# Hash attention and MLP on one Trainium2 core: attention by whole head pairs in place of half pairs

## The chip, the cores and the metric

The kernel runs on one core of one Trainium2 chip (trn2). The metric is device time in microseconds (us) of one execution, from the start of the program to its end; lower is better. The engines are called PE (TensorE, matrix products), DVE (VectorE), ACT (ScalarE), POOL (GpSimd) and SP (SyncE, which here only issues DMAs). SBUF is the on-chip memory, and PSUM is where PE writes its results; it has eight banks of 512 f32 columns on 128 partitions.

## The reference

Two stages follow each other. The first is attention with a mask by hash: each query and key gets six bits, the signs of its products with `proj`, and a query sees only the keys of its own bucket. The second is an MLP with PReLU over the attention's output, reshaped to 3072 tokens of 512.

```python
# q, k, v: (4, 8, 768, 64) f32; proj: (64, 6); w_in: (512, 2048); w_out: (2048, 512)
q_bits = (np.einsum('bhsd,dk->bhsk', q, proj) > 0)
k_bits = (np.einsum('bhsd,dk->bhsk', k, proj) > 0)
mask = q_bucket[:, :, :, None] == k_bucket[:, :, None, :]
scores = np.where(mask, scale * np.matmul(q, k.transpose(0, 1, 3, 2)), -1e9)
attn = np.exp(scores - scores.max(-1, keepdims=True))
attn = attn / (np.sum(attn, axis=-1, keepdims=True) + 1e-09)
x = np.matmul(attn, v)          # then (B,H,S,D) -> (B*S, H*D)
h = x @ w_in
out = (np.maximum(h, 0.0) + alpha * np.minimum(h, 0.0)) @ w_out
```

## The kernel before

The kernel has a fast path (`fast_path`) that always runs, and a general path that runs afterwards only if a flag says that the inputs were out of range; it doesn't run here. All that follows is the fast path. It has an attention stage of about 345 us and an MLP stage (a Winograd-like scheme of seven products in place of eight) of about 550 us.

Attention works on **head pairs**: two heads of 64 lie side by side on the 128 partitions, and there are 4 x 4 = 16 pairs. The 768 queries of a pair are cut into `NCH` = 2 chunks of `CW` = 384, and the 768 keys into `NC` = 6 blocks of 128. A **unit** `u` is one chunk of one pair (32 units); each of its steps is a function:

- `turn` (L671): six PE transposes bring q or k of a pair from tokens on partitions to head dimensions on partitions (`tr`); one copy by ACT takes them out of PSUM.
- `hash_bits` (L691): PE multiplies `tr` by `wh`, which holds `proj` in 32 columns for each head's 64 rows; each product takes the 64 rows of one head and writes 32 partitions. ACT takes the signs (DVE for k in the first pair) and writes `bits` as bf16: for each pair four instructions of 32 rows for q and three of 64 or 128 rows for k. The heads' and halves' places in PSUM are crossed (`s ^ half`), so that the eight products of a pair stand in eight different places of PE's array.
- `scores` (L730): a tile is 128 keys by 384 queries for both heads. The bit products go first (bf16, both heads side by side in PE's rows), and q times k in f32 is added to them in PSUM. ACT takes the exponential of the tile, 128x768, into one of ten `pt` tiles (L742). A key outside the bucket gets so small an exponent that its share vanishes. `two_banks` (L666) gives the PSUM tile; there are three, shared by scores, turns and bits.
- `add_first`, `add_last`, `add_total` (L749 to L760): the sum of the six `pt` tiles of a unit, tile by tile. DVE adds tiles 0 and 1 into `accp`; a DMA issued by POOL adds tile 2 to it in place; DVE adds tiles 3, 4 and 5 into `accd`, and `accp` to that.
- `attend` (L763): v transposed times the exponentials, in 32-column pieces, into one PSUM bank `av`. In chunk 0 one more column of ones gives the sum of v.
- `totals` (L776): a product of `accd` with ones gives each query's sum in a bank of its own, `sm`.
- `divide` (L786): DVE transposes these sums, takes reciprocals, POOL copies them between partitions, DVE spreads them by a second transpose and multiplies `av` by them (L811); the result `x` is stored to DRAM (`x_s`).

Beside that, attention prepares the weights: the 32 pieces of `w_in` and `w_out` come as 64-bit words and are rounded to f32 by `weight_abs` (ACT), `weight_clamp`, `weight_parts`, `weight_sum` and `weight_sums` (DVE), one piece per unit, and stored to DRAM for the MLP.

**What sets the order.** `do` keeps the compute instructions of every engine in the order in which the program calls them. The loop over units (from L1123 on) calls: the second half of this unit's score tiles, the first half of the next unit's, `divide` of the previous unit with the weight work inside it, the additions, bits of the next pair (first chunk) or turns for the pair after it (second chunk), `attend`, `totals`. So PE has six score tiles, one block of bits or turns, one v product and one block of sums per unit. DMAs are not held by `do`: the framework places those of SP and POOL on their queues by its own schedule. The tiles of `tile_pool` with `bufs=1` or 2 set which write waits for which read.

PSUM has three score tiles of two banks, one bank `av` and one bank `sm`. In the MLP, class `Product` uses `two_banks` for its bank "a", and the banks of `sm` and `av` for "b" and "c".

Of the kernel before, what the change touches and what calls it, by code (L numbers as in the profile page):

```python
# [406 lines left out]
def fast_path(  # L407
# [41 lines left out]
    attn = ctx.enter_context(ExitStack())  # L449
    pool = attn.enter_context(tc.tile_pool(name="sb", bufs=2))  # L450
# [3 lines left out]
    UNITS = NPAIR * NCH  # L454
# [4 lines left out]
    ones = const.tile([P, 32], F32, name="ones")  # L459
    wh = const.tile([P, 32], F32, name="wh")  # L460
# [6 lines left out]
    qbs = [pool.tile([P, S], BF16, name=f"qb{i}", bufs=1) for i in range(2)]  # L467
# [9 lines left out]
    NPT = 10  # L477
    pts = [pool.tile([P, 2, CW + 1], F32, name=f"pt{i}", bufs=1) for i in range(NPT)]
    n_pt = [0]

    nat, tr, bits = {}, {}, {}
    prob, accp, accd, av, vsum, sums = {}, {}, {}, {}, {}, {}
# [21 lines left out]
    def setup():  # L504
# [4 lines left out]
        for s in range(2):  # L509
            nc.sync.dma_start(wh[D * s : D * s + D, :NB], proj)  # L510
        nc.sync.dma_start(alpha16, moe_alpha.rearrange("(t p) -> t p", p=P))
        make_identity(nc, ident)
        do(DVE.memset(ones, 1.0))

        ps = psum.tile([P, 512], F32, name="nil", tag="av")
        nil.append(lambda: do(PE.matmul(ps, zero[:, :P], zero, start=True, stop=True)))
# [4 lines left out]
        for r in range(0, P, 32):  # L521
            do(DVE.memset(hb[r : r + 2 * NB], 1.0 if r % D else -1.0))
            do(DVE.memset(hb[r : r + NB], -1e-37))
# [5 lines left out]
        for t in pts:  # L529
            do(POOL.memset(t[:, :, CW : CW + 1], 1.0))  # L530
        for t in qbs:
            do(POOL.memset(t, 0.0))
# [158 lines left out]
    def hash_bits(pi, halves=BOTH, engine=None):  # L691

        if halves.start == 0:
            bits["q", pi] = qbs[pi % 2]
            bits["k", pi] = pool.tile([P, S], BF16, name=f"kb{pi}", tag="kb")
        ps = {"k": two_banks(f"hs{pi}")}
        ps["q"] = psum.tile([P, 1, 512], F32, name=f"hsq{pi}", tag="sm") if engine is DVE else ps["k"]
        for half in range(halves.start, halves.stop):  # L700
            for name in "qk" if engine is DVE else "kq":
                for s in range(2):
                    r, c = D * s, D * (s ^ half) + 32 * "kq".index(name)

                    for t, c in [("k", c)] + ([("q", c ^ D)] if engine is DVE and name == "q" else []):
                        do(PE.matmul(
                            ps[t][c : c + 32, half if t == "k" or engine is not DVE else 0, :CW], wh[r : r + D],
                            tr[name, pi][r : r + D, half * CW : (half + 1) * CW], start=True, stop=True,
                        ))
        for half in range(halves.start, halves.stop):  # L710
            cols = slice(half * CW, (half + 1) * CW)
            for s in range(2):
                c = D * (s ^ half ^ (engine is DVE)) + 32
                do(ACT.activation(  # L714
                    bits["q", pi][D * s : D * s + 32, cols], ps["q"][c : c + 32, 0 if engine is DVE else half, :CW], AF.Sign, bias=hb[c : c + 32],
                ))

            for to, c, n in [(0, 0, P)] if half == 0 else [(0, D, D), (D, 0, D)]:
                dst, src = bits["k", pi][to : to + n, cols], ps["k"][c : c + n, half, :CW]
                if engine is DVE:  # L720
                    do(DVE.tensor_scalar(
                        dst, src, hb_k[c : c + n, 0:1], hb_k[c : c + n, 1:2], op0=ALU.is_gt, op1=ALU.subtract,
                    ))
                else:
                    do(ACT.activation(dst, src, AF.Sign, bias=hb[c : c + n]))  # L725


    def scores(u, half):
        pi, g = divmod(u, NCH)
        qs = slice(g * CW, (g + 1) * CW)  # L730
        for kc in range(half * NC // 2, (half + 1) * NC // 2):
            sc = two_banks(f"sc{u}_{kc}")
            ks = slice(kc * P, (kc + 1) * P)
            for what, first in ((bits, True), (tr, False)):
                for s in range(2):
                    r = slice(D * s, D * s + D)
                    do(PE.matmul(  # L737
                        sc[:, s, :CW], what["k", pi][r, ks], what["q", pi][r, qs], start=first, stop=not first,
                    ))
            pt = pts[n_pt[0] % NPT]  # L740
            n_pt[0] += 1
            do(ACT.activation(pt[:, :, :CW], sc[:, :, :CW], AF.Exp, scale=SCALE / DOWN))  # L742
            prob[u, kc] = pt


    def p(u, kc):
        return prob[u, kc][:, :, :CW]

    def add_first(u):  # L749
        accp[u] = pool.tile([P, 2, CW], F32, name=f"accp{u}", tag="accp")  # L750
        do(DVE.tensor_tensor(accp[u], p(u, 0), p(u, 1), op=ALU.add))  # L751
        nc.gpsimd.dma_start(accp[u], p(u, 2), accum_op=ALU.add)  # L752

    def add_last(u):
        accd[u] = pool.tile([P, 2, CW], F32, name=f"accd{u}", tag="accd", bufs=1)
        do(DVE.tensor_tensor(accd[u], p(u, 3), p(u, 4), op=ALU.add))  # L756
        do(DVE.tensor_tensor(accd[u], accd[u], p(u, 5), op=ALU.add))  # L757

    def add_total(u):
        do(DVE.tensor_tensor(accd[u], accd[u], accp[u], op=ALU.add))  # L760


    def attend(u):  # L763
        pi, g = divmod(u, NCH)
        av[u] = psum.tile([P, 512], F32, name=f"av{u}", tag="av")
        w = CW + 1 if g == 0 else CW
        for kc in range(NC):
            for s in range(2):
                for t in range(0, D, 32):
                    do(PE.matmul(  # L770
                        av[u][D * s + t : D * s + t + 32, :w], nat["v", pi][:, s, kc * D + t : kc * D + t + 32],
                        prob[u, kc][:, s, :w], start=(kc == 0), stop=(kc == NC - 1),
                    ))


    def totals(u):  # L776

        sums[u] = psum.tile([P, HW2], F32, name=f"sm{u}", tag="sm")
        for s in range(2):
            for h in range(2):  # L780
                r = D * s + 32 * h
                do(PE.matmul(  # L782
                    sums[u][r : r + 32], ones, accd[u][:, s, h * HW2 : (h + 1) * HW2], start=True, stop=True,
                ))

    def divide(u, between=lambda: None):  # L786

        pi, g = divmod(u, NCH)  # L790
        b, hp = pairs[pi]
        if g == 0:
            vsum[pi] = pool.tile([P, 1], F32, name=f"vs{pi}", tag="vs")
            do(DVE.tensor_scalar(vsum[pi], av[u][:, CW : CW + 1], EPS, None, op0=ALU.mult))
        n = HW2 // 32
        a = pool.tile([P, HW2], F32, name=f"st{u}", tag="st", bufs=1)
        r = pool.tile([P, n], F32, name=f"rc{u}", tag="rc")
        rr = pool.tile([P, 2, n], F32, name=f"rr{u}", tag="rr")
        d = pool.tile([P, CW], F32, name=f"dn{u}", tag="dn", bufs=1)
        do(DVE.transpose(a, sums[u]))  # L800
        do(DVE.tensor_scalar(r, a.rearrange("p (n w) -> p n w", w=32)[:, :, 0], S * EPS, None, op0=ALU.add))
        do(DVE.reciprocal(rr, r.unsqueeze(1).to_broadcast([P, 2, n])))  # L802
        for q0 in (0, D):
            q1 = q0 + 32
            do(POOL.tensor_copy(rr[q0 : q0 + 32, 1], rr[q1 : q1 + 32, 1]))  # L805
            do(POOL.tensor_copy(rr[q1 : q1 + 32, 0], rr[q0 : q0 + 32, 0]))  # L806
        between()
        do(DVE.transpose(d, rr.rearrange("p h n -> p (h n)").unsqueeze(2).to_broadcast([P, 2 * n, 32])))

        x = mid.tile([P, CW], F32, name=f"x{u}", tag="x")  # L810
        do(DVE.scalar_tensor_tensor(x, av[u][:, :CW], vsum[pi], d, op0=ALU.add, op1=ALU.mult))  # L811
        nc.sync.dma_start(x_s[b, hp][:, g * CW : (g + 1) * CW], x)
# [25 lines left out]
    class Product:  # L838
# [9 lines left out]
        def times(self, bank, left, right, start):  # L848

            if start:  # L850
# [3 lines left out]
                else:  # L854
                    t = psum.tile([P, 512], F32, name=self.name + bank, tag="sm" if bank == "b" else "av")
# [217 lines left out]
    def verdict():  # L1073
        ps = psum.tile([4, P], F32, name="vd", tag="sm")
# [15 lines left out]

    last = UNITS - 1
    first, second = slice(0, 1), slice(1, 2)
    load_part(0, "q", slice(0, CH), nc.sync)
# [19 lines left out]
    scores(0, 0)  # L1113
# [3 lines left out]
    add_first(0)  # L1117
# [4 lines left out]
    weight_sum(0)  # L1122
    for u in range(UNITS):  # L1123
        pi, g = divmod(u, NCH)

        def weight_rest():
            weight_sum(u)
            weight_group(u)
            weight_clamp(u + 1)

        scores(u, 1)
        if u < last:
            scores(u + 1, 0)
        if u:
# [140 lines left out]
```

## Time and profile before

| what | value |
|---|---|
| time, median of three runs | 900.01 us (899.64 to 900.18) |
| time of the profiled run; span of its trace | 899.33 us; 897.5 us |
| exponentials, L742 | 192 x 813 ns |
| f32 score passes, L737 | 768 x 482 ns |
| v product passes, L770 | 1536 x 488 ns |
| bit passes, L706 | 256 x about 497 ns |
| sum passes, L782 | 256 x 326 ns |
| the three other additions on DVE, L751, L756, L757 | 32 each x 951, 949, 958 ns |
| DMA over the whole span | 146.88 MB, mean 164 GB/s |

An f32 product is two passes on PE, each of which the profile counts. A row of the profile's groups has the line, engine, operation, result and operands, shape, count, then busy time and the mean of one, then the engine's idle time ahead of it and what ended it. For PE a form such as 64*128 is the part of the array that a pass takes, rows by columns; passes in different parts run at the same time, and their recorded durations overlap, so PE's rates are read from start to start.

### The profile page before, as it was taken

To read this page: it belongs to the slowest core of one execution; us is meant where nothing else is said; L and a number is where in the kernel's file an instruction comes from. 1 tells how busy PE (TensorE), PEld (TensorE's weight loads), DVE (VectorE), ACT (ScalarE), POOL (GpSimd) and SP (SyncE) were. 2 spreads that over 40 slices of the span, in tenths; PEclk is the share of its full clock that TensorE was granted. 3 is DMA by queue.
4 is the path that set the end of the run, shared out by engine and by line. 5 is a ranking of instruction groups with operands and counts; after the bars stand their busy time and mean duration, and the time that the engine had idled before them with its cause. 6 is when DMAs were issued, how large, how long until landed. Compare 5 with 4: busy or idle time off the path is not lost.

```text
span 897.5 us, 15668 instructions
## 1 busy us (share of the span) xinstructions
PE 886.4 (99%) x5886; PEld 590.7 (66%) x5886; DVE 757.3 (84%) x1362; ACT 406.2 (45%) x726; POOL 100.4 (11%) x194
## 2 busy tenths in 40 slices
PE   9999999999999999999999999999999999999996
PEld 4444445444444445557997557997557998556996
DVE  5988988988999996899988668988668989768986
ACT  6788888888888863222112222112222111222111
POOL 1222222222232222120000000000000000000000
PEclk9999999999999999999999999999999999999999
DMA  9778888699799765478333535343525242530242
GB/s 240 183 179 184 209 222 214 169 269 275 170 233 212 186 159 175 174 275 304 123 130 99 171 98 179 101 152 86 173 97 192 95 158 78 155 120 0 95 144 71
DMA packets 131909, 146.88 MB, mean 164 GB/s; under 512 B 78304, under 2 KB 118000, under 8 KB 128240
## 3 DMA queue, kind: packets, MB, share of 16 engines
q1 hardware_dynamic: 118672, 123.90, 44.5%
q0 software_dynamic: 11008, 20.97, 11.7%
q8 instruction: 48, 0.79, 0.4%
q10 hardware_dynamic: 2144, 0.92, 0.4%
q14 instruction: 37, 0.30, 0.1%
HBM read 104.87 MB, written 28.31 MB: 148 GB/s over the span
## 4 chain that ended last, share of the span: by engine, by line
PE 89%; DVE 7%; DMA 2%; issue 1%; SPq 1%; ACT 0%; DVEq 0%; ACTq 0%
PE sc L737 17%; PE av L770 14%; PE f_0a L858 2%; PE z_3a L858 2%; PE z_6a L858 2%; PE z_5a L858 2%; PE f_2a L858 2%; PE f_1a L858 2%; PE z_2a L858 2%; PE f_3a L858 2%; PE z_7a L858 2%; PE z_1a L858 2%; PE z_4a L858 2%; PE f_7a L858 2%; PE f_6a L858 2%; PE f_5a L858 2%
## 5 line engine op out<-in xcount | busy, mean ns | idle before, releaser
L742 ACT ACTIVATE pt<-sc 128x768 f32<-128x768 f32 x192 | 153.6, 813 | 48.5 <-PE sc L737 46.7
L737 PE MATMUL sc<-qT,kT 64*128 64x384 f32 x768 | 155.2, 482 | 0.0
L770 PE MATMUL av<-pt,vn 128*32 128x384 f32 (+1 forms) x1536 | 130.6, 488 | 0.5 <-DVE x L811 0.5
L770 PEld LDWEIGHTS av<-pt,vn 128*32 128x32 f32 x1536 | 46.6, 109 | 75.7 <-issue 71.1
L737 PEld LDWEIGHTS sc<-qT,kT 64*128 64x128 f32 x768 | 68.2, 188 | 35.8 <-issue 35.6
L911 DVE TENSOR_TENSOR g<-g,g 128x384 f32<-128x384 f32 x128 | 68.4, 555 | 2.2
L737 PE MATMUL sc<-qb,kb 64*128 64x384 bf16 x384 | 63.3, 324 | 0.1
L752 POOL DMA_DIRECT2D accp<-pt x32 | 38.6, 1205 | 194.3 <-issue 78.6
L975 DVE TENSOR_TENSOR gs<-g,gs 128x768 f32<-128x768 f32 x56 | 53.4, 953 | 1.0
L967 DVE TENSOR_TENSOR ws<-wl 128x512 f32<-128x512 f32 x56 | 38.5, 688 | 17.7 <-DMA wl<-w_out_s 16.1
L975 DVE TENSOR_TENSOR gs<-g 128x768 f32<-128x768 f32 x56 | 53.3, 953 | 0.0
L907 DVE SCALAR_TENSOR_TENSOR g<-h,alpha 128x384 f32<-128x384 f32 x32 | 19.7, 616 | 26.4 <-ACT h L900 26.4
L737 PEld LDWEIGHTS <-kb 64*128 64x128 bf16 x384 | 18.8, 94 | 30.6 <-issue 9.2
L760 DVE TENSOR_TENSOR accd<-accd,accp 128x768 f32<-128x768 f32 x32 | 30.7, 958 | 7.7 <-DMA accp<-pt 6.8
L714 ACT ACTIVATE qb<-hs,hb 32x384 bf16<-32x384 f32 x60 | 34.4, 574 | 1.1
L757 DVE TENSOR_TENSOR accd<-accd,pt 128x768 f32<-128x768 f32 x32 | 30.7, 958 | 3.3
L751 DVE TENSOR_TENSOR accp<-pt,pt 128x768 f32<-128x768 f32 x32 | 30.4, 951 | 0.0
L756 DVE TENSOR_TENSOR accd<-pt,pt 128x768 f32<-128x768 f32 x32 | 30.4, 949 | 0.0
L806 POOL COPY rr<-rr 32x6 f32<-32x6 f32 x64 | 27.5, 430 | 2.6
L805 POOL COPY rr<-rr 32x6 f32<-32x6 f32 x64 | 19.8, 310 | 61.6 <-DVE rr L802 60.3
L725 ACT ACTIVATE kb<-hs,hb 64x384 bf16<-64x384 f32 (+1 forms) x45 | 26.0, 578 | 0.6
L800 DVE STREAM_TRANSPOSE st<-sm 128x192 f32<-128x192 f32 x32 | 12.2, 381 | 14.0 <-PE sm L782 13.8
(350 smaller groups left out, 1824.6 us busy)
## 6 DMA issues: line engine op xcount, KB each, us to landing
wi<-w_in_s SPq DMA_DIRECT2D x32, 896.0 KB, 4.7
wl<-w_out_s SPq DMA_DIRECT2D x16, 1024.0 KB, 4.8
accp<-pt POOLq DMA_DIRECT2D x32, 384.0 KB, 5.2
wl<-w_out_r SPq DMA_DIRECT2D x12, 1024.0 KB, 4.9
raw<-in_moe_w_out_dram SPq DMA_DIRECT2D x16, 512.0 KB, 5.2
raw<-in_moe_w_in_dram SPq DMA_DIRECT2D x16, 512.0 KB, 5.0
w_in_s<-wsi SPq DMA_DIRECT2D x16, 448.0 KB, 5.8
vn<-in_v_dram SPq DMA_DIRECT2D x16, 384.0 KB, 6.0
```

The source lines that it names most:

```text
L714: do(ACT.activation(bits["q", pi][D * s : D * s + 32, cols], ps["q"][c : c + 32, 0 if engine is DVE else half, :CW], AF.Sign, bias=hb[c : ...
L737: do(PE.matmul(sc[:, s, :CW], what["k", pi][r, ks], what["q", pi][r, qs], start=first, stop=not first,))
L742: do(ACT.activation(pt[:, :, :CW], sc[:, :, :CW], AF.Exp, scale=SCALE / DOWN))
L751: do(DVE.tensor_tensor(accp[u], p(u, 0), p(u, 1), op=ALU.add))
L752: nc.gpsimd.dma_start(accp[u], p(u, 2), accum_op=ALU.add)
L757: do(DVE.tensor_tensor(accd[u], accd[u], p(u, 5), op=ALU.add))
L760: do(DVE.tensor_tensor(accd[u], accd[u], accp[u], op=ALU.add))
L770: do(PE.matmul(av[u][D * s + t : D * s + t + 32, :w], nat["v", pi][:, s, kc * D + t : kc * D + t + 32], prob[u, kc][:, s, :w], start=(kc = ...
L858: do(PE.matmul(self.ps[bank], self.left(left, k), self.right(right, k), start=start and k == 0, stop=k == self.nk - 1, skip_group_check=no ...
L911: do(DVE.tensor_tensor(new_g(b, to)[:, i], g_m[b, x][:, i], g_m[b, y][:, i], op=ALU.subtract))
L967: do(DVE.tensor_tensor(t, w2[b, n, x], w2[b, n, y], op=op))
L975: do(DVE.tensor_tensor(t, g2[b, n, x], g2[b, n, y], op=ALU.subtract))
```

## The change

A pair is now one step: the loop runs over 16 pairs and handles both chunks together.

- All 12 score tiles of a pair follow each other, in the order key block by key block with both chunks of each. `pts` is now six tiles, one per key block, which hold both chunks; there is one set of them.
- Then follow both turns for pair + 2, the bits of pair + 1, the v product of both chunks, the sums of both chunks.
- `av` has two banks, one per chunk, from a pool of its own that is closed with the attention stage. The sums no longer have a bank: they go into columns 400 to 495 of `av`'s banks. Each group of 32 partitions takes two quarters of a chunk's sums there, 96 columns each, by two products with `ones` that is one in 16 of its 32 columns and zero in the others, the second added to the first.
- `hash_bits` multiplies all 128 rows at once: `wh` has two versions, each with zeros in the other head's rows. The places are no longer crossed. ACT takes q's signs for both heads and both chunks in one instruction of 128x768, and k's in two of 32x768. The tile with zeros between its bits is now k's (`kbs`), not q's.
- The additions are 1536 wide, four on DVE and one by DMA for each pair; `accp` and `accd` have one buffer each. In `divide` the spreading transpose and the multiply are 768 wide, and x is stored by one DMA.
- Weight work is done for two pieces per pair, spread between these steps.
- In the MLP, banks "b" and "c" come from a new pool that takes the place of `av`'s.

The diff, cut to its core:

```diff
+    psum_av = attn.enter_context(tc.tile_pool(name="psa", bufs=1, space=bass.MemoryType.PSUM))
...
-    pts = [pool.tile([P, 2, CW + 1], F32, name=f"pt{i}", bufs=1) for i in range(NPT)]
+    pts = [pool.tile([P, NCH, 2, CW + 1], F32, name=f"pt{i}", bufs=1) for i in range(NC)]
...
-            nc.sync.dma_start(wh[D * s : D * s + D, :NB], proj)
+            nc.sync.dma_start(wh[D * s : D * s + D, s, :NB], proj)
...
         for half in range(halves.start, halves.stop):
-            for name in "qk" if engine is DVE else "kq":
+            for n, name in enumerate("qk"):
                 for s in range(2):
-                    r, c = D * s, D * (s ^ half) + 32 * "kq".index(name)
...
+                    c = D * s + 32 * n
+                    w = D if engine is DVE and name == "q" else 32
+                    do(PE.matmul(
+                        ps[name][c : c + w, half, :CW], wh[:, s, :w], tr[name, pi][:, half * CW : (half + 1) * CW],
+                        start=True, stop=True,
+                    ))
...
+        do(ACT.activation(
+            cells(bits["q", pi], slice(0, P)), ps["q"][:, halves, :CW], AF.Sign, bias=hb,
+        ))
+        for s in range(2):
+            c = D * s + 32
+            dst, src = cells(bits["k", pi], slice(D * s, D * s + 32)), ps["k"][c : c + 32, halves, :CW]
...
+                do(ACT.activation(dst, src, AF.Sign, bias=hb[c : c + 32]))
...
-            do(ACT.activation(pt[:, :, :CW], sc[:, :, :CW], AF.Exp, scale=SCALE / DOWN))
+            do(ACT.activation(pts[kc][:, g, :, :CW], sc[:, :, :CW], AF.Exp, scale=SCALE / DOWN))
...
+    def add_first(pi):
+        accp[pi] = pool.tile([P, 2 * NCH, CW], F32, name=f"accp{pi}", tag="accp", bufs=1)
+        do(DVE.tensor_tensor(accp[pi], p(0), p(1), op=ALU.add))
+        nc.gpsimd.dma_start(accp[pi], p(2), accum_op=ALU.add)
...
+        for g in range(NCH):
+            for e in range(2):
+                for s in range(2):
+                    for h in range(2):
+                        r = D * s + 32 * h
+                        do(PE.matmul(
+                            av[pi][r : r + 32, g, SUMS : SUMS + QW], ones[:, e],
+                            accd[pi][:, NCH * g + s, h * HW2 + e * QW : h * HW2 + (e + 1) * QW],
+                            start=e == 0, stop=e == 1, skip_group_check=True,
+                        ))
...
+        x = mid.tile([P, NCH, CW], F32, name=f"x{pi}", tag="x", bufs=1)
+        do(DVE.scalar_tensor_tensor(x, av[pi][:, :, :CW], vsum[pi], d, op0=ALU.add, op1=ALU.mult))
+        nc.sync.dma_start(x_s[b, hp], x.rearrange("p g w -> p (g w)"))
...
-                    t = psum.tile([P, 512], F32, name=self.name + bank, tag="sm" if bank == "b" else "av")
+                    t = psum_bc[0].tile([P, 512], F32, name=self.name + bank, tag=bank)
...
+        scores(pi, [c for c in CELLS if pi or c not in ahead])
+        if pi:
+            divide(pi - 1, weight_begin)
+        add_first(pi)
+        weight_sum(i)
+        weight_group(i)
+        load_weight(i + 3)
...
+        weight_clamp(i + 1)
+        add_last(pi)
+        weight_parts(i + 1)
+        weight_sum(i + 1)
+        weight_group(i + 1)
+        load_weight(i + 4)
+        add_total(pi)
+        weight_sums(2)
+        if pi + 2 < NPAIR:
+            turn(pi + 2, "q")
+            turn(pi + 2, "k")
+        if pi + 1 < NPAIR:
+            hash_bits(pi + 1)
+        attend(pi)
+        if pi + 1 == NPAIR:
             now = ff1(0, 0)
             now.step(1)
             now.step(5)
...
+        totals(pi)
+        if pi + 1 == NPAIR:
+            divide(pi)
```

## The prediction, made before the changed kernel was run

> **What bounds the kernel now.** I read the page's busy lines first, then busy time by stretch, then TensorE's (PE's) own waits, and last its order of time through one head pair.
>
> ```profile
> span 897.5 us, 15668 instructions
> PE 886.4 (99%) x5886; PEld 590.7 (66%) x5886; DVE 757.3 (84%) x1362; ACT 406.2 (45%) x726; POOL 100.4 (11%) x194
> ...
> 150.00:317.00 167.00, 167.00 (x1705) 81.31 (x1700) 152.25 (x280) 144.02 (x217) 43.27 (x80) 1.00 0.83 211
> ...
> PE sm L782 <- DVE accd L760: 0.9, 1, 0.9
> PE av L770 <- DVE x L811: 0.5, 1, 0.5
> ```
>
> The stretch 150 to 317 us holds eight head pairs of the attention stage. Its columns are PE, weight loads, VectorE (DVE), ScalarE (ACT), GpSimd (POOL), granted clock, DMA share, GB/s. PE is busy for all of 167.00 us; DVE for 91%, ACT for 86%, DMA for 83%. The last two lines are all that PE waited for in attention once it ran: 1.4 us, both in the first pairs. So the stage lasts as long as PE's instruction stream, and the other three have slack of about 2 to 3 us per pair. A pair takes 167.00/8 = 20.87 us. Its stream (one later half of a pair, then the first half of the next):
>
> ```profile
> 150.09 0.51 PE L782 MATMUL sm<-accd,ones 128*32 128x192 f32 x8
> 150.53 0.34 PE L737 MATMUL sc<-qb,kb 64*128 64x384 bf16 x2
> 150.70 0.81 PE L737 MATMUL sc<-qT,kT 64*128 64x384 f32 x4
> ...
> 154.58 0.33 PE L737 MATMUL sc<-qb,kb 64*128 64x384 bf16 x2
> 155.48 0.88 PE L678 MATMUL tp_q<-ident,qn 128*128 128x128 f32 x6
> ...
> 156.94 4.08 PE L770 MATMUL av<-pt,vn 128*32 128x384 f32 x48
> 160.83 0.51 PE L782 MATMUL sm<-accd,ones 128*32 128x192 f32 x8
> 161.27 0.34 PE L737 MATMUL sc<-qb,kb 64*128 64x384 bf16 x2
> ...
> 166.22 0.51 PE L706 MATMUL hs<-kT,wh 64*32 64x384 f32 x2
> ...
> 166.57 0.49 PE L706 MATMUL hs<-kT,wh 64*32 64x384 f32 x2
> ...
> 167.03 1.18 PE L770 MATMUL av<-pt,vn 128*32 128x385 f32 x12
> ```
>
> Durations overlap, so I use start to start. Six score tiles: 155.48 - 150.53 = 4.95. Turns: 156.94 - 155.48 = 1.46. V product of a chunk: 160.83 - 156.94 = 3.89 (the other chunk 3.90). Sums: 161.27 - 160.83 = 0.44. Bits: 167.03 - 166.22 = 0.81. A pair is 2 x 4.95 + 1.46 + 0.81 + 2 x 3.90 + 2 x 0.44 = 20.85, as found.
>
> Inside a block the rates are plain. A score tile repeats after (154.58 - 150.53)/5 = 0.81. In the v product 48 passes in column groups of 32 go in rounds of four: 3.89/12 = 0.324 per round, which is 0.84 ns a column. The 192-column sums are two rounds of half that, 0.325; the 0.44 shows 0.115 between blocks. Twelve transposes of 128 columns at 0.84 are 1.30, block 1.46: again about 0.12 to 0.16. The bits' 16 passes of 384 columns take only two rounds (starts at 166.22 and 166.57), eight at once.
>
> **What the Trainium skill says.** "TensorEngine Tiling (Array Packing)", section "Tiling Modes", lists 128x32 as four independent tiles and 64x32 as eight. The trace agrees: four v passes per 0.324 us, eight bit passes per 0.33. Its "Key Properties" say that a change of mode drains the array. The trace agrees where it can show it: v product to sums, both 128*32, loses nothing (3.89 is twelve rounds), while each change of mode costs about 0.12. "DMA: Bandwidth & Descriptors", section "Issuing engines are not separate DMA queues", says that all issuers share 16 engines; the DMA share of 0.83 in the stretch fits, and makes the larger accumulating transfer the doubtful one.
>
> **The change, part by part (PE, the path).**
>
> *Bits.* The weight is now 128 rows high with zeros for the other head, so the mode goes from 64*32 to 128*32. The passes stay 16 of 384 columns, but four fit at once: 4 x 0.324 = 1.30 in place of 0.65. Cost +0.65 per pair. Bounds: 0 if eight still ran at once, +0.77 with a drain behind it.
>
> *Order and modes.* Now: scores, turns, v, sums, scores, bits, v, sums: six mode changes. Then: 12 score tiles (64*128), turns (128*128), bits, v, sums (all 128*32): three. Gain 3 x 0.12 = -0.36. Bounds -0.25 (bits to v not seamless) and -0.45.
>
> *Sums.* Sixteen passes of 192 columns become 32 of 96: eight rounds of 0.081 = 0.65, as now 2 x 0.325. Nothing here shows 96 columns; transposes of 128 columns follow at 0.109, their full streaming rate, so weight loads are hidden to that size. At 0.109 a round the cost would be 8 x 0.028 = +0.22. I take 0.
>
> Scores and v product keep passes and shapes: 0. By the blocks: 4.95 + 6 x 0.81 = 9.80, turns 1.46, bits 1.30, v 24 x 0.324 = 7.78, sums 0.65 + 0.115: 21.10 against 20.85, **+0.25 per pair**. Fourteen pairs make bits for the next: +3.5. The last has no bits and saves two changes: -0.2.
>
> **What lies beside it.** Per pair on DVE, four additions of 1536 take the place of eight of 768:
>
> ```profile
> L760 DVE TENSOR_TENSOR accd<-accd,accp 128x768 f32<-128x768 f32 x32 | 30.7, 958 | 7.7 <-DMA accp<-pt 6.8
> ...
> accp<-pt POOLq DMA_DIRECT2D x32, 384.0 KB, 5.2
> ```
>
> The 384-wide addition of the second stage takes 555 ns (its row), so the slope is 1.04 ns a column and 1536 take about 1.75 us: 4 x 0.16 = 0.65 saved. The wider transpose and multiply of the division save some 0.3 more. ACT loses four 32-row and three other sign operations (7 x 0.58) and gets one of 128x768 and two of 32x768 (0.81 each): -1.6. Neither bounds, so this is worth nothing to the span; PE at 167.00 of 167.00 hides it.
>
> The waits are new. Set t = 0 at the pair's first score matmul. DVE: division 0.2 + 2 x (0.38 + 0.17 + 0.23), in it the weight's first half 2.3, then 1.0 + 1.0 for the wide transpose and multiply, to about 6.3 with the start (v's banks are needed at 12.6), first addition to 8.1, weight work to 10.1, two additions to 13.6, weight work to 16.5, total to 18.2. PE wants the sums at 9.80 + 1.46 + 1.30 + 7.78 = 20.3: 2.1 us spare. The accumulating DMA, now 768 KB and 512 packets, may land up to 10.4 us after the first addition before PE waits. It took 5.2 for half, of which POOL's issue was 1.2; doubling all gives 10.4, doubling issue and transfer but not latency some 8. Just inside. On ACT the 12 exponentials at 0.81 keep pace with 0.81 a tile and three buffers; turns and signs follow. Behind them the magnitudes end at about t = 18, and only then may q and k three pairs ahead load; SP issues them beside v and weight loads, with 6 us to landing, at about t = 24 to 26 against a need at 21 + 9.8. POOL's copies precede its DMA and end by t = 4. All hidden, with less room than now.
>
> **Start.** The first bit products on DVE's path are 64 and 32 columns wide in turn (+0.65 each, two calls), and k's signs become two instructions of 0.68 for one: scores start about 1.0 later than the present 8.3. Against that go the two waits above (1.4) and four mode changes. Adding up to the end of the first pair's sums I get 33.4 to 35.4, depending on k of pair 2 and on the first DMA; the same work now ends at about 36.05 less three tiles, 33.6. Take +0.5 (-0.5 to +2).
>
> **End.** The MLP's second bank now comes out of the pair's v banks, free when the division's last multiply ends. From the sums' end that takes 0.25 (release) + 0.8 + 0.8 + 1.0 (POOL) + 1.0 + 1.0 = 4.9 us; PE has three products of 1.29 (3.9) ahead of it. +0.9 (0 to 2). The MLP itself is untouched.
>
> Sum: 3.5 - 0.2 + 0.5 + 0.9 = **+4.7 us** on the span of 897.5. The profiled run's own time was 899.33, the three runs 899.64 to 900.18, so I add it to 900.0: about 904.8.
>
> **Rivals.**
> A, other side: the bits stay cheap. If passes of half-zero 128-row weights also went eight at once, the pair would lose only mode changes: -0.36 to -0.45 and, with 15 pairs, about 895. It decides below a bit block of 1.0 us. For it: 0.65 now. Against it: the v product has the new shape and never shows more than four per 0.324. 6%.
> B, a wait takes over: the doubled accumulating DMA lands later than 10.4 us after the addition. Each microsecond beyond costs 16: landing at 11.5 gives 920. For it: DMA share 0.83, the longest landing 9.9 for half the size, and DVE did wait for it six times (6.8 us). Against: most landings near 5. 12%.
> C, q and k land after the turn wants them: bursts of weight loads in the middle pairs, 2 to 5 us in one to three pairs: 908 to 915. 8%.
> D, no change: start and end come out at their low bounds and drains at 0.15: +1. 8%.
>
> **The numbers.** My case 66%, own range 902 to 909; A 6, B 12, C 8, D 8. 0.2% (1.8 us) is about what a measurement of this kernel can tell from no change. Faster 0.06, same 0.08, slower 0.86. Eight in ten lie between 901.5 and 914: A below, most of B above.
>
> **What would show it.** Bit block at 1.3 us with four passes per round; 12 tiles in 9.8; no gap between bits, v and sums; period 21.1; PE still busy throughout; DVE's share down to some 85%. Wrong if bits take 0.65, or if PE waits for the total, for the banks of v, or for q and k at the turns.

## The result, and the profile after

The changed kernel took 914.1 us (912.8 to 914.96, 6 runs) against 899.83 us before on the same chip (899.34 to 901.17, 6 runs): a ratio of 1.0156, 95% interval 1.0143 to 1.017. It is slower, as forecast, but by 14.3 us and not by 4.7; 914.1 lies just above the range's end of 914.0. The profiled run, 912.8 us, was the fastest of the six; its span grew from 897.5 to 911.0 us, by 13.5, and it is these 13.5 us that the traces explain.

PE's order of time through one pair after the change; columns are start, duration, engine, line, operation, result and operands, part of the array, shape, count:

```profile
160.05 0.34 PE L735 MATMUL sc<-qb,kb 64*128 64x384 bf16 x2
...
169.84 0.88 PE L679 MATMUL tp_q<-ident,qn 128*128 128x128 f32 x6
...
171.30 0.52 PE L706 MATMUL hs<-qT,wh 128*32 128x384 f32 x2
171.31 0.52 PE L706 MATMUL hs<-kT,wh 128*32 128x384 f32 x2
171.65 0.49 PE L706 MATMUL hs<-qT,wh 128*32 128x384 f32 x2
171.66 0.49 PE L706 MATMUL hs<-kT,wh 128*32 128x384 f32 x2
171.97 0.49 PE L706 MATMUL hs<-qT,wh 128*32 128x384 f32 x2
...
172.29 0.49 PE L706 MATMUL hs<-qT,wh 128*32 128x384 f32 x2
...
172.62 3.74 PE L768 MATMUL av<-pt,vn 128*32 128x385 f32 x44
```

Start to start: 12 score tiles 9.79, turns 1.46, bits 1.32 in four rounds (171.30, 171.65, 171.97, 172.29) and the v product right behind the fourth. The pair before gives the rest:

```profile
151.52 7.94 PE L768 MATMUL av<-pt,vn 128*32 128x385 f32 x96
159.27 0.85 PE L784 MATMUL av<-accd,ones 128*32 128x96 f32 x32
```

V product 159.27 - 151.52 = 7.75, sums 160.05 - 159.27 = 0.78. A pair is 9.79 + 1.46 + 1.32 + 7.75 + 0.78 = 21.10 us. The forecast was 21.10, and each of its blocks is within 0.03 us of these. So the steady pair is not where the time went. PE's waits show where it did (waiter, what it waited for, us in total, times, longest), together with the tile `accp`, asked for in the stretch 180 to 215 us:

```profile
PE av L784 <- DVE accd L755: 6.9, 2, 6.6
...
L747 POOL DMA_DIRECT2D accp<-pt x1: 1282/1282/1282, 188.7 to 188.7; - x1
...
  DVE accd L755: 9.5, 1
...
DMA to landing us min/median/max: 17.7/17.7/17.7
```

In pair 8 (counted from 0) the sums (L784) waited for the total, and the total had waited 9.5 us for the accumulating DMA, which was issued at 188.7 and landed 17.7 us later. Over the whole run the median of its landings is 9.3 us. The 6.6 us of PE's wait count from the recorded end of the last v pass; from start to start the sums, which began at 208.23, came 6.8 us late (208.23 - 193.72 - 7.75, where 193.72 is the start of pair 8's v product). What shared the 16 DMA engines with it is in SP's order of time:

```profile
188.62 0.91 SPq L846 DMA_DIRECT2D wi<-w_in_s  x2
189.62 0.43 SPq L568 DMA_DIRECT2D raw<-in_moe_w_in_dram  x1
190.27 0.65 SPq L846 DMA_DIRECT2D wi<-w_in_s  x1
```

These are the first three loads of the MLP's weights, 896 KB each. The program calls two of them in pair 9 and one in pair 12; the framework, which places SP's DMAs by its own schedule, put all three into pair 8, within 2 us of the accumulating DMA. That is not new: the kernel before issues the same three loads one behind the other in the same pair. Here are that line of SP's order of time, and the landings of its four accumulating DMAs (384 KB each) in the stretch 180 to 215 us:

```profile
191.97 7.02 SPq L836 DMA_DIRECT2D wi<-w_in_s  x3
...
DMA to landing us min/median/max: 4.5/7.8/9.9
```

The one issued at 190.5, just ahead of the loads, took 8.5 us to land and the next, at 201.4, took 9.9, the longest of that whole run, against a median of 5.2. PE waited for neither.

In the changed kernel the wait had a sequel. Busy time by stretch (length, then PE, weight loads, DVE, ACT, POOL, clock, DMA share, GB/s):

```profile
201.90:204.00 2.10, 0.00 (x0) 0.00 (x0) 0.00 (x0) 0.02 (x1) 0.00 (x0) 1.00 1.09 318
...
205.50:206.00 0.50, 0.00 (x0) 0.00 (x0) 0.00 (x0) 0.00 (x0) 0.00 (x0) 0.74 1.24 298
206.00:208.00 2.00, 0.00 (x0) 0.00 (x0) 1.58 (x1) 0.00 (x0) 0.00 (x0) 0.50 0.87 197
208.00:212.50 4.50, 4.27 (x44) 2.76 (x46) 2.73 (x13) 0.81 (x1) 1.27 (x4) 0.50 0.36 109
212.50:214.00 1.50, 1.50 (x12) 0.80 (x10) 1.47 (x2) 1.01 (x2) 0.00 (x0) 0.98 0.04 11
```

PE's granted clock falls to one half between 205.5 and 206 and is back at about 212.5. By then PE works again, at half speed: the sums of pair 8 take 1.44 us in place of 0.78, and the next twelve score tiles 11.21 in place of 9.79.

The 13.5 us, from the two traces: start -0.9 (the first pair's sums end at 32.75; the same work ended at 33.6 before), steady pairs and last pair +3.5, wait in pair 8 +6.8, half clock +2.1 (0.66 + 1.42), a wait of 0.5 in pair 2, end +1.5.

### The profile page after: what moved, and what is told of

Same layout as the page of the kernel before. It is cut to its first block, busy times and chain, and to the rows that moved or that the text cites. A ratio compares the mean times of both kernels' runs of the same rounds, so it can differ in the third digit from the quotient of the medians.

```text
span 911.0 us, 15799 instructions
## 1 busy us (share of the span) xinstructions
PE 893.1 (98%) x6134; PEld 603.8 (66%) x6134; DVE 741.6 (81%) x1269; ACT 386.8 (42%) x664; POOL 54.4 (6%) x110
## 4 chain that ended last, share of the span: by engine, by line
PE 52%; DVE 6%; DMA 1%; issue 1%; SPq 0%; ACT 0%; DVEq 0%; POOL 0%; ACTq 0%
PE z_5a L868 2%; PE z_3a L868 2%; PE z_6a L868 2%; PE f_2a L868 2%; PE f_1a L868 2%; PE z_2a L868 2%; PE f_3a L868 2%; PE z_7a L868 2%; PE f_0a L868 2%; PE z_1a L868 2%; PE z_4a L868 2%; PE f_7a L868 2%; PE f_6a L868 2%; PE f_5a L868 2%; PE f_4a L868 2%; PE z_2c L868 1%
## 5 line engine op out<-in xcount | busy, mean ns | idle before, releaser
L768 PE MATMUL av<-pt,vn 128*32 128x385 f32 (+1 forms) x1536 | 127.0, 485 | 0.0
L755 DVE TENSOR_TENSOR accd<-accd,accp 128x1536 f32<-128x1536 f32 x16 | 28.1, 1758 | 27.6 <-DMA accp<-pt 27.6
L751 DVE TENSOR_TENSOR accd<-pt,pt 128x1536 f32<-128x1536 f32 x16 | 28.1, 1758 | 4.4 <-ACT pt L738 4.4
L752 DVE TENSOR_TENSOR accd<-accd,pt 128x1536 f32<-128x1536 f32 x16 | 28.1, 1758 | 1.7
L746 DVE TENSOR_TENSOR accp<-pt,pt 128x1536 f32<-128x1536 f32 x16 | 28.0, 1750 | 0.4 <-ACT pt L738 0.4
L724 ACT ACTIVATE kb<-hs,hb 32x768 bf16<-32x768 f32 x30 | 26.8, 894 | 0.6
L747 POOL DMA_DIRECT2D accp<-pt x16 | 20.6, 1290 | 90.8 <-ACT pt L738 73.4
L706 PE MATMUL hs<-qT,wh 128*32 128x384 f32 (+1 forms) x128 | 24.0, 493 | 0.0
L868 PE MATMUL f_0a<-x,wi 128*128 128x384 f32 x64 | 23.5, 489 | 0.0
L868 PE MATMUL f_5a<-x,wi 128*128 128x384 f32 x64 | 23.3, 486 | 0.0
```

The lines of the kernel that those rows point to most:

```text
L724: do(ACT.activation(dst, src, AF.Sign, bias=hb[c : c + 32]))
L746: do(DVE.tensor_tensor(accp[pi], p(0), p(1), op=ALU.add))
L751: do(DVE.tensor_tensor(accd[pi], p(3), p(4), op=ALU.add))
L752: do(DVE.tensor_tensor(accd[pi], accd[pi], p(5), op=ALU.add))
L755: do(DVE.tensor_tensor(accd[pi], accd[pi], accp[pi], op=ALU.add))
L768: do(PE.matmul(av[pi][D * s + t : D * s + t + 32, g, :w], nat["v", pi][:, s, kc * D + t : kc * D + t + 32], pts[kc][:, g, s, :w], start=(k ...
```

## The experiments

Each was measured together with the kernel before, to which its ratio refers: 899.6 us for runs 1 to 4 (898.8 to 900.8), 899.28 for runs 5 to 8 (898.38 to 901.35). The brackets behind a ratio are its 95% interval.

**1. The third addition on VectorE.**

```diff
-        nc.gpsimd.dma_start(accp[pi], p(2), accum_op=ALU.add)
+        do(DVE.tensor_tensor(accp[pi], accp[pi], p(2), op=ALU.add))
```

> The third addition goes to VectorE instead of the accumulating DMA. Theory (one late landing of that DMA in pair 8, 6.8 us of PE's wait, 2.1 us of half clock after it, and 0.5 us in pair 2 are what lies above the forecast): all three go, 914.1 - 9.4 = 904.7, and no wait of PE for the total is over 0.3 us. Rival (VectorE is short of time by now, and the DMA was the cheaper way): 1.75 us more per pair on VectorE make the total late in every pair by up to 1 us, 914 to 921.

Measured: 905.05 us (903.31 to 906.24), ratio 1.0055 (1.0035 to 1.0074). PE has no wait for the total in its trace, the pair repeats every 21.10 us and the clock stays whole. This is 9.0 us less than 914.1, close to the 9.4 of the theory. VectorE had the time: it is busy for 156.00 of 167.00 us in the stretch 150 to 317.

**2. The three weight loads one by one.** Each is held by a write of VectorE into its buffer, behind the total of its pair.

```diff
+            if gate:
+                do(DVE.memset(w_m[n][:, 0, 0, 0:1], 0.0))
...
         add_total(pi)
+        if 0 <= pi - NI - 1 < 3:
+            load_w(pi - NI - 1, gate=True)
...
-            load_w(0)
-            load_w(1)
...
-        if i == HW + 8:
-            load_w(2)
```

> The three loads of the MLP's first weights (896 KB each), which started together in pair 8, are held until the total of pairs 9, 10 and 11 is made, one in each; the accumulating DMA stays 768 KB. Theory (it was late because it started together with these loads): its longest landing falls from 17.7 us to 12 or less, PE waits at most 1 us, half clock disappears, 905 (904.5 to 906.5). Rival (768 KB are late by themselves, as soon as anything else is under way): a wait of several us stays somewhere, 910 to 915.

Measured: 904.29 us (903.54 to 905.32), ratio 1.0051 (1.0034 to 1.0067). PE's wait for the total and the landings of the accumulating DMA, over the whole run:

```profile
PE av L784 <- DVE accd L755: 1.3, 2, 1.0
...
DMA to landing us min/median/max: 7.4/9.4/12.2
```

The 768 KB went on by DMA, and its median landing is as before, 9.4 us; only the 17.7 is gone. The longest, 12.2, is a little over the 12 expected; it came in pair 4, where none of the three loads is, and PE waited 1.0 us there. So size alone brings short waits, but not the long one.

**3. Half of the third addition by DMA, the burst left in place.**

```diff
-        nc.gpsimd.dma_start(accp[pi], p(2), accum_op=ALU.add)
+        nc.gpsimd.dma_start(accp[pi][:, :NCH], p(2)[:, :NCH], accum_op=ALU.add)
+        do(DVE.tensor_tensor(accp[pi][:, NCH:], accp[pi][:, NCH:], p(2)[:, NCH:], op=ALU.add))
```

> Only chunk 0 of the third addition is done by DMA (384 KB as before the change), chunk 1 on VectorE; the three weight loads stay together. Theory (it takes both, the burst and the doubled size): landing 10 to 12 us in pair 8 instead of 17.7, PE waits 1 us or less, 905 to 906.5. Rival (the burst alone delays any DMA that starts with it): landing 14 us or more, PE waits 3 us or more with half clock behind it, 909 to 913.

Measured: 905.89 us (904.64 to 908.07), ratio 1.0074 (1.0053 to 1.0095). The same two lines of its trace:

```profile
PE av L785 <- DVE accd L756: 1.4, 1, 1.4
...
DMA to landing us min/median/max: 4.4/4.6/12.6
```

Next to the same loads 384 KB landed in 12.6 us at most, a little above what was expected, and PE waited 1.4 us, a little more than the 1 us allowed. With this short wait the clock stayed whole. So the burst alone doesn't bring the long wait either: it took both. The two add up: the loads made the landing about 8 us longer at either size (17.7 against 9.3, 12.6 against the median 4.6), and the doubled size about 5 us. By what means the loads delay the DMA is not shown; in the changed kernel the DMA share was 1.00 to 1.09 from 190 to 201.5 us.

**4. The old bits in the changed kernel.** `hash_bits`, `wh`, `hb` and the zeroed tile are those of the kernel before; the first pair's q product on VectorE's path takes a bank of `av`.

```diff
-                        ps[name][c : c + w, half, :CW], wh[:, s, :w], tr[name, pi][:, half * CW : (half + 1) * CW],
+                            ps[t][c : c + 32, half if t == "k" or engine is not DVE else 0, :CW], wh[r : r + D],
+                            tr[name, pi][r : r + D, half * CW : (half + 1) * CW], start=True, stop=True,
```

> The bits are made as before the change (64 rows at a time, crossed places, seven sign instructions on ScalarE); all else as changed. Theory (four passes at once in place of eight cost 1.31 - 0.81 = 0.51 us in each of 14 pairs, plus some 1 us at the start): 906.0 (905 to 907) with the wait in pair 8 unchanged. Rival (ScalarE's shorter work pays for it, since its 1.6 us more per pair now delay the exponentials): 912 to 916.

Measured: 907.0 us (906.85 to 909.49), ratio 1.0081 (1.0064 to 1.0097). The pair falls to 20.62 us, 0.48 less, and the bit block to 0.81. But PE came sooner to a total that came no sooner:

```profile
PE av L786 <- DVE accd L757: 9.6, 4, 7.5
...
DMA to landing us min/median/max: 6.7/9.9/18.1
```

The long wait in pair 8 is there again with half clock behind it, now 7.5 us, and waits of about a microsecond appear in pairs 2 and 4. The traced run, 909.49 us, was the slowest of four, the other three lie within 0.3 us of 907. The theory's sum holds to 1 us, though the wait did not stay unchanged, as it assumed; the rival's doesn't hold. In this trace a faster pair makes the DMA's landing dearer.

**5. Old bits and the third addition on VectorE.** The edits of 1 and 4.

> The changed kernel with the old bits and the third addition on VectorE, so without accumulating DMA. Theory (the change is pair order, 0.22 us a pair won; bits, 0.48 lost; and the DMA's waits): the pair repeats every 20.62 us and 905.05 - 14 x 0.48 - 1 = 897.3, 0.2 to 0.4% under the kernel before. Rival (with a shorter pair, VectorE's 18.8 us of work make the total late): the pair repeats at 20.9 or more, 900 or above.

Measured: 897.97 us (896.99 to 901.46), ratio 0.9989 (0.9981 to 0.9997). Most pairs repeat at 20.62; the total is late twice, by 0.8 us together, with VectorE now busy for 158.84 of 167.00 us. It is 0.1% under the kernel before, less than the 0.2 to 0.4% expected, a gain of 1.3 us where single runs of that kernel lie up to 3.0 us apart.

**6. Old bits and the loads one by one.** The edits of 2 and 4.

> The changed kernel with the old bits and the three weight loads held one by one, 768 KB by DMA. Theory: no long wait and no half clock, but the total is wanted 0.5 us sooner in each pair, so the DMA's 9.4 us to landing show as waits of 0.2 to 1.3 us in five or so pairs: 897 + 2 to 4 = 899 to 901. Rival (the waits seen with the old bits came from the burst as well): 897 to 898.

Measured: 900.1 us (898.13 to 902.95), ratio 1.0007 (1.0 to 1.0013). The landing's median is 9.9 us and its longest 11.4; PE waits 1.8 us in three pairs for the total, and 1.6 us in one for the write right behind the total that holds a load. In that one too the total had waited for the DMA, and the write followed it at once. This is the theory's range, and the burst is gone: at 20.62 us a pair, 768 KB by DMA come too late in some pairs.

**7. Old bits, loads one by one, half of the addition by DMA.** The edits of 2, 3 and 4.

> As the last one, but only chunk 0 of the third addition is done by DMA. Theory: landing near 4.6 us, no wait of PE in a steady pair, 20.62 us a pair, 897 (896.5 to 898). Rival (something other than the accumulating DMA holds the sum): no better than the last one.

Measured: 895.81 us (895.29 to 896.83), ratio 0.9963 (0.995 to 0.9977): faster than both kernels. The landing's median is 4.7 us, from the sums of the third pair to those of the fourteenth each pair repeats at 20.61 or 20.62, and PE fills the stretch again:

```profile
150.00:317.00 167.00, 167.00 (x1860) 85.03 (x1856) 153.34 (x247) 146.86 (x222) 19.73 (x40) 1.00 0.75 204
```

It is 1.2 us better than the theory's 897 and below its range. The last stores would account for most of this: from PE's last pass to the end 7.0 us go by, and 7.9 in run 5, whose loads stay together.

**8. The new bits alone, in the kernel before.** `hash_bits`, `wh`, `hb` and the zeroed tile are those of the changed kernel; k's bank on VectorE's path is `sm`.

```diff
-                            ps[t][c : c + 32, half if t == "k" or engine is not DVE else 0, :CW], wh[r : r + D],
-                            tr[name, pi][r : r + D, half * CW : (half + 1) * CW], start=True, stop=True,
+                        ps[name][c : c + w, 0 if engine is DVE and name == "k" else half, :CW], wh[:, s, :w], tr[name, pi][:, half * CW : (half + 1) * CW],
+                        start=True, stop=True,
```

> The kernel before with the new bits alone (128 rows at a time, four passes at once, three sign instructions). Theory (0.65 us more per pair, less one change of mode between bits and v product, 0.12 to 0.14): 14 to 15 times 0.51 is 7.4, and 1 to 1.5 at the start: 908 (907 to 909). Rival (the shorter work of ScalarE is worth something in the half-pair order): 904 or less.

Measured: 906.98 us (905.99 to 908.52), ratio 1.0085 (1.0071 to 1.0099). PE's order of time in it:

```profile
148.30 0.52 PE L705 MATMUL hs<-qT,wh 128*32 128x384 f32 x2
...
149.62 4.06 PE L768 MATMUL av<-pt,vn 128*32 128x385 f32 x48
```

The bit block is 1.32 us against 0.81 before, and the pair 21.33 against 20.85, +0.48: the same term from the other side. ScalarE's shorter work bought nothing.

## Why the prediction was wrong

The direction, the path of a steady pair and its length were right. The step that failed is the landing of the accumulating DMA: it was called "just inside" and priced at zero for all pairs, and in pair 8 it cost 6.8 us of wait and 2.1 us of half clock behind it, 8.9 of the 13.5.

- **Bits.** Forecast +0.65, four rounds of 0.324 and no drain behind them. The block shows four rounds and 1.32 us; runs 4 and 8 price the form at 0.48 us a pair net, one mode change included.
- **Order and modes.** With the old bits the pair order alone gives 20.62 against 20.85 (run 4), -0.23 for two changes of mode saved; with the new bits three are saved and the pair is 21.10, +0.25. Both are what the block sums say. So the change of mode, at some 0.12 each, fits as the reason that the order wins anything (no run varies it alone), and it is smaller than what the bits lose.
- **Sums.** Taken at no extra; two sums blocks before were 0.88, one is now 0.78, against 0.77 forecast. Eight rounds of 0.081 and one change of mode make that, so passes of 96 columns stream as the wider ones do.
- **The accumulating DMA.** This is the failed step. The landing in a quiet pair was well placed (8 to 10.4 us forecast, 9.3 median), and so, nearly, was the limit. In pair 8 PE wanted the sums at 193.72 + 7.75 = 201.47 and the total takes 1.76, so the DMA had until 199.7: 11.5 us after the first addition's end at 188.15, where 10.4 was forecast, and 11.0 after its issue. It took 17.7, 6.7 too long. What was wrong was to compare the limit with twice the median landing. The landings of 8.5 and 9.9 beside and behind the loads stood in the trace of the kernel before; doubled as the prediction doubled 5.2, they would have given 17 to 20 us, past the limit. The prediction quoted the 9.9 in rival B and set it aside as rare ("most landings near 5"). It named bursts of weight loads in rival C, and held them against the loads of q and k alone. Runs 2 and 3 show that burst and size had to meet.
- **Rival B** named the right wait, but priced it as one of all 16 pairs; it came in one (and for 0.5 us in pair 2), and cost 8.9 us with its sequel.
- **The half clock** was no term of the sum. Its 2.1 us follow from the wait and went with it (runs 1, 2 and 3).
- **Start** came out at -0.9 against +0.5 (-0.5 to +2): k of pair 2 had landed and the first total was not late. In the runs with the new bits it lay between -0.9 and +0.5.
- **End** was +1.5 against +0.9: the product that needs bank "b" moved back by 0.5, as forecast in kind; the other 1.0 comes later: 0.2 in the MLP and 0.8 in the last stores. From PE's last pass to the end 8.0 us go by, 7.3 before; in the other runs with the pair order these are 7.9 to 8.1 where the three loads stay together and 7.0 to 7.4 where they are held. Why the last stores follow the loads of pair 8 stays open.

Without the wait and its sequel the forecast holds: runs 1 and 2 take 905.05 and 904.29 us, forecast 904.8 (its terms add up to 904.7). That it is so close is in part luck: start and end were each off, by -1.4 and +0.6 in the first trace, and partly cancel.

## What to carry to other kernels

When a change doubles a transfer and halves its slack, compare the slack with the worst landing beside the largest burst of the whole run, not with the median; and look in the trace that you have where the framework really places loads that the program calls later: both stood there. A PE shape that is two times as high for the same output can cost half of the passes that run at once: count rounds before trading PE time for fewer instructions on an engine that isn't the bound. If both the order and the operations of a stage change, price them apart: here the order was worth 0.23 us a pair and the operations cost 0.48.

## What the runs showed of the hardware

- PE's half clock follows waits of 6.6 us (the changed kernel) and 7.5 us (run 4), and none of 1.4 (run 3) or 1.6 us (run 6). In the changed kernel it sets in 4.1 us after the last pass of the v product has ended (201.65) and ends 4.3 us after PE works again (208.23); in run 4 these are 3.0 and 5.8 us (the clock read in stretches of 0.25 and 0.5 us). "TensorE: Matmul & The Clock Gate" in the Trainium skill, section "What's actually happening", says that a window of about 3.4 us without activity halves the clock and one of sustained activity restores it. The four times are of that order and not equal to it. The half clock itself lasts 6.83 us in one trace and 10.24 in the other, two and three times 3.41, as it would if the clock changed only at the borders of such windows; two cases don't prove it. Such a wait costs more than its length: 2.1 us on 6.8 here, 2.8 on 7.5 in run 4.
- Transfers of 768 KB took 9.3 us in the median beside the usual traffic, and one took 17.7 beside 2.7 MB more. 384 KB beside the same loads took 12.6, against a median of 4.6.
